# Attention followed by a mixture of experts on one core: a new order of loads, deferred VectorE work and smaller preparation steps

## Chip, cores, metric

One core of one Trainium2 chip. The metric is the device time of one execution in microseconds (us). Every profile is one execution, and its span is about 1.8 us shorter than the time reported for the same run. In the lines of the profile PE is TensorE, PEld its weight loads, DVE VectorE, ACT ScalarE, POOL GpSimd, and SP the engine that only issues transfers; a `q` behind a name means its queue. An eviction is the copy or sum that takes a product out of the banks that TensorE writes. "Loss" below means this, for any stretch: the start-to-start distances of the matmuls that the trace records, minus what these matmuls take at their usual pace (216 ns for 256 columns, 109 ns for 128, 54.5 ns for the half-size ones). That pace sums to 1198.4 us over the whole kernel, before and after alike.

## The reference, cut

```python
def _attn_ref(q, k, v, lam):                    # (4, 8, 768, 64) each; lam (8,)
    for b in range(nb):                         # blocks of 64 positions, with a running state
        intra = np.einsum('bhic,bhjc->bhij', qb, kb) * Dmask[None]
        intra = np.einsum('bhij,bhjd->bhid', intra, vb)
        inter = np.einsum('bhid,bhde->bhie', qb * lam_pow[None], kv_state)
        out[:, :, sl] = intra + inter
        kv_state = lam_block[None, :, None, None] * kv_state + np.einsum('bhsd,bhse->bhde', kb_dec, vb)

def _moe_ref(x, domain_probs, w1, w2):          # x (3072, 512); w1 (4, 512, 1024); w2 (4, 1024, 512)
    p = domain_probs / (domain_probs.sum(-1, keepdims=True) + 1e-09)
    for e in range(E):
        h = np.maximum(x @ w1[e], 0.0)
        out += p[:, e:e + 1] * (h @ w2[e])
```

## The kernel before

Attention runs in 24 chunks of 128 positions, eight to a group. A chunk has three parts: `turn` (transposes of q and k), `scores`, and `values` (with the update of the state `kv`). The experts' products use seven half-size products in place of eight (M1 to M7), so sums of blocks of x and of the weights have to be made first. For the first two experts of group 0 these products work straight from SBUF (`direct_product`, four "quarters" each). For all others the operands are made by GpSimd (group 0's x by VectorE) and ScalarE's queue stores them in DRAM ahead of time ("chores"); SP's queue loads them back (`xs_in`, `ws_in`). VectorE sums that are not urgent wait in a list, `background`, and one is issued after each part of a product.

The parts that the change touches (cuts marked `...`):

```python
    def load(n):
        ...
        for name, src in (("q", q), ("k", k), ("v", v)):
            x = small(f"{name}n")[:].rearrange("p (h d) -> p h d", d=D)
            nc.sync.dma_start(out=x, in_=src[b, :, c * C:(c + 1) * C, :].rearrange("h p d -> p h d"))
    ...
    lam_bc = consts.tile([P, H], FP32, name="lam_bc")
    nc.scalar.dma_start(out=lam_bc[:], in_=lam.partition_broadcast(P))
    lam_hp = consts.tile([P, NHP], FP32, name="lam_hp")
    for hd in range(2):
        nc.scalar.dma_start(
            out=lam_hp[half[hd], :], in_=lam.rearrange("(hp hd) -> hd hp", hd=2)[hd].partition_broadcast(D),
        )
    ...
    def pump():                                  # one chore; stores of the chore before are issued first
        for f in stores:
            f()
        stores.clear()
        if chores:
            chores.pop(0)()

    def inner(eng, what, to, blk, ops, at):      # the sums of one operand, then three stores
        ...
        stores.append(lambda: (
            nc.scalar.dma_start(out=to[:, 0], in_=blk[:, 0, 0:256]),
            nc.scalar.dma_start(out=to[:, 1:5], in_=s[:]),
            nc.scalar.dma_start(out=to[:, 5:7], in_=blk[:, 1].rearrange("p (a f) -> p a f", a=2)),
            made.add(what),
        ))
    ...
    for n in range(4):
        load(n)
    for name in ("A21", "A22", "A11"):
        raw_w1(0, name)
    probs = consts.tile([P, NTOK // P, E], FP32, name="probs")
    nc.scalar.dma_start(out=probs[:], in_=moe_domain_probs.rearrange("(t p) e -> p t e", p=P))
    ...
    # in values(): the state, at once after its product
            for hd in range(2):
                ...
                    tt(nc.vector, kv[sl, :, sl], kv[sl, :, sl], q_decay[...], ALU.mult)
                    tt(nc.vector, kv[sl, :, sl], kv[sl, :, sl], kpv[sl, :, sl], ALU.add)
    ...
    # in first_product(): an eviction, then (as a later step) the sums that wait in background
            at, begins = READ[i]
            if not begins:
                tt(nc.vector, new[at][:], p[:], new[at][:], ALU.add)
            elif old is None:
                nc.scalar.copy(out=new[at][:], in_=p[:])
            else:
                tt(nc.vector, new[at][:], p[:], old[at][:], ALU.add)
    ...
    # in second_product(): the result of the last expert, 128 x 512
            if e == E - 1 and m in ("M5", "M3"):
                nc.gpsimd.dma_start(out=out[n * P:(n + 1) * P, :], in_=acc.pop(n)[0][:])
    ...
    # the main loop, after each of four parts x of a pair of products (cut)
                rest()
                ...
                if x in (1, 4, 6):
                    pump()
```

Of the kernel before, what the change touches and what calls it, by code (L numbers as in the profile page):

```python
# [20 lines left out]
def kernel(  # L21
# [36 lines left out]
    C = P  # L58
# [39 lines left out]
    def load(n):  # L98
        b, c = divmod(n, NCH)
        tiles = []  # L100
        for name, src in (("q", q), ("k", k), ("v", v)):
            x = small(f"{name}n")[:].rearrange("p (h d) -> p h d", d=D)
            nc.sync.dma_start(out=x, in_=src[b, :, c * C:(c + 1) * C, :].rearrange("h p d -> p h d"))  # L103
            tiles.append(x)
        nat[n] = tiles
# [3 lines left out]
    lam_hp = consts.tile([P, NHP], FP32, name="lam_hp")  # L109
    for hd in range(2):  # L110
        nc.scalar.dma_start(
            out=lam_hp[half[hd], :], in_=lam.rearrange("(hp hd) -> hd hp", hd=2)[hd].partition_broadcast(D),
        )
# [56 lines left out]
    def prepare_w1(e):  # L170
        st = {}

        def block(name, i, j):
            t = stage.tile([P, 2, W], FP32, name="w1b", tag="st")
            src = moe_w1[e, j * 256:(j + 1) * 256, i * W:(i + 1) * W]
            nc.sync.dma_start(out=t[:], in_=src.rearrange("(c p) f -> p c f", p=P))
            st[name] = t

        def total(name, a, b, op):
            t = stage.tile([P, 2, W], FP32, name="w1o", tag="st")  # L180
            tt(nc.gpsimd, t[:], st[a][:], st[b][:], op)
            st[name] = t

        def ready(m):
            inner_w1(e, m, st[A_OF[m]])

        return [
            lambda: (block("A11", 0, 0), block("A21", 1, 0), block("A22", 1, 1)),
            lambda: ready("M1"),
            lambda: (total("S1", "A21", "A22", ALU.add), ready("M5")),  # L190
            lambda: (total("S3", "A11", "A21", ALU.subtract), ready("M7")),
            lambda: (total("S2", "S1", "A11", ALU.subtract), block("A12", 0, 1), ready("M6")),
            lambda: ready("M2"),
            lambda: (total("S4", "A12", "S2", ALU.subtract), ready("M3")),
            lambda: ready("M4"),
        ]
# [39 lines left out]
    def prepare_x(g):  # L236

        st = {}

        def total(name, a, b, op):  # L240
            t = stage.tile([P, 2, W], FP32, name="xo", tag="st")
            tt(nc.gpsimd, t[:], a, b, op)
            st[name] = t[:]

        def ready(m, blk):
            inner_x(nc.gpsimd, g, m, blk)

        return [lambda: ready("M1", b11), lambda: ready("M2", b21)], [
            lambda: (total("T1", b12, b11, ALU.subtract), ready("M5", st["T1"])),
            lambda: (total("T2", b22, st["T1"], ALU.subtract), ready("M6", st["T2"])),  # L250
            lambda: (total("T3", b22, b12, ALU.subtract), ready("M7", st["T3"])),
            lambda: ready("M3", b22),
            lambda: (total("T4", b21, st["T2"], ALU.subtract), ready("M4", st["T4"])),
        ]
# [29 lines left out]
    for n in range(4):  # L284
        load(n)
    for name in ("A21", "A22", "A11"):
        raw_w1(0, name)
    probs = consts.tile([P, NTOK // P, E], FP32, name="probs")
    nc.scalar.dma_start(out=probs[:], in_=moe_domain_probs.rearrange("(t p) e -> p t e", p=P))
# [16 lines left out]
    nc.vector.tensor_copy(out=q_decay[:, :, 0], in_=lam_hp[:])  # L306
# [11 lines left out]

    gate = consts.tile([P, NTOK // P, E], FP32, name="gate")
# [15 lines left out]

    def turn(n, tags):
        qn, kn, _ = nat[n]
# [11 lines left out]
        if n % NCH:  # L349
            qs = small("qs")  # L350
            tt(nc.vector, qs[:], qT[:], q_decay[:].rearrange("p h c -> p (h c)"), ALU.mult)
# [7 lines left out]
    def scores(n, tags):  # L359
        qT, kT, _ = turned[n]  # L360

        sp = [bank(tags[hd], "sp") for hd in range(2)]
        for hp in range(NHP):
            for hd in range(2):
                nc.tensor.matmul(  # L365
                    out=sp[hd][:, hp * C:(hp + 1) * C], lhsT=hc(kT)[half[hd], hp], rhs=hc(qT)[half[hd], hp],
                    start=True, stop=True,
                )
        st = [small("st") for _ in range(2)]
        for hd in range(2):  # L370
            tt(nc.vector, st[hd][:], sp[hd][:], s_decay[:, hd].rearrange("p h c -> p (h c)"), ALU.mult)
        masked[n] = st

    def values(n, tags):
        _, kn, vn = nat.pop(n)
# [18 lines left out]
        if not last:  # L394
# [7 lines left out]
            for hd in range(2):  # L402
                sl = half[hd]
                if first:
                    nc.vector.tensor_copy(out=kv[sl, :, sl], in_=kpv[sl, :, sl])
                else:
# [4 lines left out]
                    tt(nc.vector, kv[sl, :, sl], kv[sl, :, sl], kpv[sl, :, sl], ALU.add)  # L411

# [21 lines left out]
    background = []  # L434

    def rest(n=1):
        for _ in range(min(n, len(background))):
            background.pop(0)()

# [134 lines left out]
    def second_product(g, e, m, banks):  # L574

        def part(sj, s):
# [29 lines left out]
            if e == E - 1 and m in ("M5", "M3"):  # L606
                nc.gpsimd.dma_start(out=out[n * P:(n + 1) * P, :], in_=acc.pop(n)[0][:])  # L607
# [16 lines left out]
    def direct_product(e, m, blocks, tags):  # L624
# [6 lines left out]
        def quarter(at):  # L631
# [9 lines left out]
            new[at] = small("m" + at) if m in ("M1", "M2", "M5") else blocks[old][at]  # L641
            if old is None:
                nc.scalar.copy(out=new[at][:], in_=p[:])
            else:
                tt(nc.vector, new[at][:], p[:], blocks[old][at][:], ALU.add)
# [7 lines left out]
    between, blocks = [], {}  # L653
    for i in range(CPG + 2):
        if i == 3:
            sum_w1(0, "S1", "A21", "A22", ALU.add)
            sum_w1(0, "S3", "A11", "A21", ALU.subtract)
        if i == 4:
# [3 lines left out]
        if i > 4:  # L662
            pump()
        if i == 6:
            between = direct_product(0, "M1", blocks, ("g1", "g3"))
        for f, lag in ((scores, 1), (turn, 0), (values, 2)):
# [3 lines left out]
            if i == 7 and lag == 0:  # L670
                between += direct_product(0, "M2", blocks, ("g1", "g3"))
            if between:
                between.pop(0)()
        if i + 4 < CPG:
            load(i + 4)
        if i == 0:
            raw_w1(0, "A12")
        if i == 6:
            gates()

    def sum_x(name, a, b):
        t = stream.tile([P, 7, 256], FP32, name="xt", tag="xw"[len(x_now) % 2])
        x_now[name] = t[:, 0:4].rearrange("p (c a) t -> p c (a t)", c=2)
        tt(nc.vector, x_now[name], x_now[a], x_now[b], ALU.subtract)

    sum_x("T1", "B12", "B11")
    sum_x("T2", "B22", "T1")
    sum_x("T3", "B22", "B12")
    sum_x("T4", "B21", "T2")
    for f in between:  # L690
        f()
    chores.extend(lambda n=n: raw_w1(1, n) for n in ("A11", "A12", "A21", "A22"))
    chores.append(lambda: sum_w1(1, "S1", "A21", "A22", ALU.add))
    for m in SEQ0[2:]:
# [9 lines left out]
        lambda: sum_w1(1, "S3", "A11", "A21", ALU.subtract), own[1], w2_steps[0],  # L704
        lambda: sum_w1(1, "S4", "A12", "S2", ALU.subtract), own[2], w2_steps[1],
        own[3], w2_steps[2], w2_steps[3], own[4], w2_steps[4], w1_steps[0], own[5], *w1_steps[1:3], own[6], *w1_steps[3:],
# [6 lines left out]
    for at, (g, e) in enumerate(units):  # L713
# [9 lines left out]
        for i in range(7):  # L723
# [11 lines left out]
            for x, part in enumerate(order):  # L735
# [10 lines left out]
                if x in (1, 4, 6):  # L746
                    pump()
    assert not (background or chores or stores or acc)
# [28 lines left out]
```

## Time and profile before

| | before |
|---|---|
| time, median of 3 runs | 1261.21 us (1259.52 to 1261.83) |
| span of the profile | 1257.4 us |
| matmuls at their usual pace | 1198.4 us |
| first matmul starts | 4.69 us |
| loss before 120 us | 24.8 us |
| loss from 120 to 720 us | 24.8 us, of which TensorE idle 9.7 |
| last matmul's start to the end | 5.3 us |

Read it from the top: TensorE is the bound, so a change that doesn't touch the matmuls can win only what the last four rows hold, and not all of that.

### The profile page before, as it was taken

The numbers are of one execution on the slowest core, as the hardware profiler recorded it, in microseconds if no ns is written. First come the engines' busy times: TensorE is split into PE (matmuls) and PEld (weight loads), VectorE is DVE, ScalarE is ACT, GpSimd is POOL, SyncE is SP. The second block draws the span as 40 slices with busy tenths as digits, with TensorE's granted clock in tenths as the row PEclk, the third lists the DMA queues.
The fourth block names the chain that finished last, engine by engine and source line by source line (L and its number), as shares of the span: only waits on it lengthen the run. The fifth ranks groups of instructions, "written<-read, shape, count | busy, mean of one in ns | idle before, by whom it ended". The sixth has DMA issues, their size and how long they took to land.

```text
span 1257.4 us, 16224 instructions
## 1 busy us (share of the span) xinstructions
PE 1226.8 (98%) x6376; PEld 1071.3 (85%) x6376; DVE 762.4 (61%) x1267; ACT 217.1 (17%) x361; POOL 301.1 (24%) x294
## 2 busy tenths in 40 slices
PE   6989999999999999999999999999999999999998
PEld 5878888888888888888888888888888888888887
DVE  4656478477467745756764674674764755755742
ACT  2213102111202211220221021120120120220100
POOL 3620236586356683112000700000010000000001
PEclk9999999999999999999999999999999999999999
DMA  9741477999999799667544764454565445454412
GB/s 187 209 151 47 166 251 270 374 317 382 307 341 348 225 328 362 214 222 237 176 176 151 265 232 177 175 202 154 217 224 199 178 174 203 154 217 156 167 59 93
DMA packets 173052, 273.10 MB, mean 217 GB/s; under 512 B 87600, under 2 KB 120496, under 8 KB 172976
## 3 DMA queue, kind: packets, MB, share of 16 engines
q1 hardware_dynamic: 143808, 212.37, 50.6%
q10 hardware_dynamic: 27248, 53.41, 11.3%
q0 software_dynamic: 1920, 6.29, 1.3%
q8 instruction: 50, 0.82, 0.3%
q14 instruction: 26, 0.21, 0.1%
HBM read 212.39 MB, written 59.64 MB: 216 GB/s over the span
## 4 chain that ended last, share of the span: by engine, by line
PE 47%; issue 42%; DMA 5%; POOL 2%; SPq 2%; DVE 1%; ACT 0%; ACTq 0%; POOLq 0%; DVEq 0%
PE q L589 18%; PE pg L537 14%; PE pM L637 7%; PE op L389 2%; PE sp L365 2%; PE kvp L398 2%; SPq L103 1%; PE op L383 1%; DMA xs_in<-x_ops 1%; DMA x_ops<-xo 1%; DMA w2t<-in_moe_w_dram 1%; POOL ops L93 1%; POOL out_dram L607 1%; PE qp L342 1%; DMA kn<-in_k_dram 1%
## 5 line engine op out<-in xcount | busy, mean ns | idle before, releaser
L537 PE MATMUL pg<-xs_in,ws_in 128*128 128x256 f32 x1960 | 470.9, 380 | 6.6 <-DVE m L93 3.4
L537 PEld LDWEIGHTS pg<-xs_in,ws_in 128*128 128x128 f32 x1960 | 369.2, 190 | 60.3 <-DVE m L93 5.6
L589 PE MATMUL q<-w2t,hS 128*128 128x256 f32 x1536 | 361.0, 379 | 0.0
L93 DVE TENSOR_TENSOR m<-pg,m 128x512 f32<-128x512 f32 x410 | 280.1, 688 | 92.9 <-PE pg L537 79.2
L589 PEld LDWEIGHTS q<-w2t,hS 128*128 128x128 f32 x1536 | 291.1, 190 | 39.9
L605 DVE SCALAR_TENSOR_TENSOR acc<-q,gate,acc 128x256 f32<-128x256 f32 x288 | 138.9, 482 | 234.6 <-PE q L589 234.2
L589 PE MATMUL q<-w2t,m 128*128 128x256 f32 x1152 | 270.7, 379 | 0.0
L589 PEld LDWEIGHTS q<-w2t,m 128*128 128x128 f32 x1152 | 218.5, 190 | 29.7
L607 POOL DMA_DIRECT2D out_dram<-acc x24 | 13.2, 550 | 548.6 <-DVE acc L605 548.6
L549 ACT ACTIVATE m<-m 128x512 f32<-128x512 f32 x120 | 75.4, 630 | 361.9 <-DVE m L93 349.7
L93 DVE TENSOR_TENSOR hS<-m,m 128x512 f32<-128x512 f32 x96 | 68.8, 719 | 20.9 <-ACT m L549 20.9
L545 ACT COPY m<-pg 128x512 f32<-128x512 f32 x80 | 46.5, 585 | 174.9 <-PE pg L537 157.1
L93 DVE TENSOR_TENSOR m<-m,m 128x512 f32<-128x512 f32 x96 | 73.8, 773 | 0.0
L93 POOL TENSOR_TENSOR kn<-kn,s_decay 128x256 f32<-128x256 f32 x40 | 30.1, 773 | 114.1 <-PE kp L342 110.9
L491 ACT ACTIVATE m<-m 128x512 f32<-128x512 f32 x48 | 29.9, 629 | 152.3 <-DVE m L93 147.7
L637 PE MATMUL pM<-xt,w1o 128*128 128x256 f32 x192 | 45.6, 391 | 4.8 <-DVE xt L93 3.3
L637 PEld LDWEIGHTS pM<-xt,w1o 128*128 128x128 f32 x192 | 37.2, 196 | 10.7 <-DVE xt L93 3.5
L602 DVE TENSOR_SCALAR acc<-q,gate 128x256 f32<-128x256 f32 x48 | 23.1, 482 | 37.2 <-PE q L589 37.1
L93 DVE TENSOR_TENSOR m<-pM,m 128x512 f32<-128x512 f32 x40 | 27.4, 687 | 24.9 <-PE pM L637 24.8
L93 DVE TENSOR_TENSOR st<-sp,s_decay 128x512 f32<-128x512 f32 x48 | 30.8, 684 | 11.4 <-PE sp L365 11.2
L93 DVE TENSOR_TENSOR hS<-hS,m 128x512 f32<-128x512 f32 x48 | 35.3, 736 | 0.5
L93 POOL TENSOR_TENSOR w2o<-w2b 128x1024 f32<-128x1024 f32 x8 | 18.9, 2364 | 69.4 <-DMA w2b<-in_moe_w_dram 49.9
(65 smaller groups left out, 777.4 us busy)
## 6 DMA issues: line engine op xcount, KB each, us to landing
xs_in<-x_ops SPq DMA_DIRECT2D x70, 896.0 KB, 4.6
ws_in<-w_ops SPq DMA_DIRECT2D x70, 896.0 KB, 6.6
w2t<-w_sums SPq DMA_DIRECT2D x96, 256.0 KB, 6.4
w2t<-in_moe_w_dram SPq DMA_DIRECT2D x72, 256.0 KB, 6.6
w_ops<-ops ACTq DMA_DIRECT2D x28, 512.0 KB, 6.8
x_ops<-ops ACTq DMA_DIRECT2D x21, 512.0 KB, 5.0
w2b<-in_moe_w_dram SPq DMA_DIRECT2D x32, 256.0 KB, 5.6
w_sums<-w2o ACTq DMA_DIRECT2D x16, 512.0 KB, 6.7
```

Source lines behind the costliest of these rows:

```text
L93: eng.tensor_tensor(out=o, in0=a, in1=b, op=op)
L365: nc.tensor.matmul(out=sp[hd][:, hp * C:(hp + 1) * C], lhsT=hc(kT)[half[hd], hp], rhs=hc(qT)[half[hd], hp], start=True, stop=True,)
L389: nc.tensor.matmul(out=op[half[hd], hp * C:(hp + 1) * C], lhsT=vn[:, 2 * hp + hd], rhs=hc(st[hd])[:, hp], start=(first and hp == 0), stop= ...
L398: nc.tensor.matmul(out=kpv[:, hp], lhsT=kn[:, 2 * hp:2 * hp + 2].rearrange("p h d -> p (h d)"), rhs=vn[:, 2 * hp:2 * hp + 2].rearrange("p ...
L491: nc.scalar.activation(out=o[:], in_=o[:], func=AF.Relu)
L537: nc.tensor.matmul(out=p[:, j * 256:(j + 1) * 256], lhsT=ws[:, W1_AT[i], j * P:(j + 1) * P], rhs=xs[:, X_AT[i]], start=(fresh and j == 0), ...
L545: nc.scalar.copy(out=new[at][:], in_=p[:])
L549: nc.scalar.activation(out=new[at][:], in_=new[at][:], func=AF.Relu)
L589: nc.tensor.matmul(out=p[:, s * DH:(s + 1) * DH], lhsT=h[A_OF[m]][:, c * 256 + s * P:c * 256 + (s + 1) * P], rhs=fed2[g, e, m][uu][:, c], ...
L605: nc.vector.scalar_tensor_tensor(out=o, in0=x, scalar=w, in1=o, op0=ALU.mult, op1=ALU.add)
L607: nc.gpsimd.dma_start(out=out[n * P:(n + 1) * P, :], in_=acc.pop(n)[0][:])
L637: nc.tensor.matmul(out=p[:, s * 256:(s + 1) * 256], lhsT=a[c][:, f:f + P], rhs=b[:, c, j * 256:(j + 1) * 256], start=(s == 0 and c == 0), ...
```

## The change

The intent has five parts, named as in the prediction:

- (a) **Loads.** The small strided load `lam_hp` goes (its values are copied from `lam_bc`), `probs` is loaded later, and q and k of the first two chunks come ahead of v.
- (b) **Early quarters.** The quarters of M1 and M2 are spread over the first attention group from the fifth chunk on, so that one is left to run behind the eighth chunk, while VectorE forms the sums of x.
- (c) **`soon`.** VectorE's masks, `qs` and state updates are put at the head of the deferred list, so that the next eviction is ahead of them. (For the first eight chunks they still run at once.)
- (d) **Steps.** Preparation sums and operands become separate chores, and a chore is asked for (a "pump") four times per product in place of three; most of group 0's own operands come ahead of the w2 sums.
- (e) **Results** are stored by halves, the last four halves from SP's queue.

```diff
-    lam_hp = consts.tile([P, NHP], FP32, name="lam_hp")
-    for hd in range(2):
-        nc.scalar.dma_start(
...
-            lambda: (total("T1", b12, b11, ALU.subtract), ready("M5", st["T1"])),
+            lambda: total("T1", b12, b11, ALU.subtract), lambda: ready("M5", st["T1"]),
... (every sum and its operand in the same way)
-    for n in range(4):
-        load(n)
-    for name in ("A21", "A22", "A11"):
-        raw_w1(0, name)
-    probs = consts.tile([P, NTOK // P, E], FP32, name="probs")
-    nc.scalar.dma_start(out=probs[:], in_=moe_domain_probs.rearrange("(t p) e -> p t e", p=P))
+    for n, names in ((0, "qk"), (1, "qk"), (0, "v"), (2, "qk"), (1, "v")):
+        load(n, names)
+    raw_w1(0, "A11")
+    load(3, "qk")
... (v2, A12, v3, A21, A22)
+    def soon(n, *work):
+
+        background[0:0] = work
+        if n < CPG:
+            rest(len(work))
...
-            tt(nc.vector, qs[:], qT[:], q_decay[:].rearrange("p h c -> p (h c)"), ALU.mult)
+            soon(n, lambda: tt(nc.vector, qs[:], qT[:], q_decay[:].rearrange("p h c -> p (h c)"), ALU.mult))
... (the two masks and the two state updates in the same way)
-            if e == E - 1 and m in ("M5", "M3"):
-                nc.gpsimd.dma_start(out=out[n * P:(n + 1) * P, :], in_=acc.pop(n)[0][:])
+            if e == E - 1 and m in ("M2", "M4", "M5", "M3"):
+                queue = nc.sync if (g, m) == (NG - 1, "M3") else nc.gpsimd
+                queue.dma_start(out=out[n * P:(n + 1) * P, j * DH:(j + 1) * DH], in_=o)
...
+    m1, m2 = (direct_product(0, m, blocks, ("g1", "g3")) for m in ("M1", "M2"))
+    between = {
+        4: (m1[0], m1[2]), 5: (m2[0], m2[2]), 6: (m1[1],), 7: (m1[3],), 8: (m2[1],), 9: (lambda: None, lambda: None, m2[3]),
+    }
...
+            if i == 9 and lag == 2:
+                x_sums()
...
+        if i == 5:
+            nc.scalar.dma_start(out=probs[:], in_=moe_domain_probs.rearrange("(t p) e -> p t e", p=P))
+        if i == 9:
             gates()
...
-        lambda: sum_w1(1, "S3", "A11", "A21", ALU.subtract), own[1], w2_steps[0],
-        lambda: sum_w1(1, "S4", "A12", "S2", ALU.subtract), own[2], w2_steps[1],
-        own[3], w2_steps[2], w2_steps[3], own[4], w2_steps[4], w1_steps[0], own[5], *w1_steps[1:3], own[6], *w1_steps[3:],
+        lambda: sum_w1(1, "S3", "A11", "A21", ALU.subtract), own[1], own[2],
+        lambda: sum_w1(1, "S4", "A12", "S2", ALU.subtract), own[3], own[4], *w2_steps[:2], own[5], *w2_steps[2:], own[6],
+        *w1_steps,
...
-                if x in (1, 4, 6):
+                if x % 2 == 0:
                     pump()
```

## The prediction

> **What bounds the kernel now.** I read the page's head and slices first, then busy times by stretch, then the timeline wherever TensorE was idle, and last every matmul's start.
>
> ```profile
> span 1257.4 us, 16224 instructions
> PE 1226.8 (98%) x6376; PEld 1071.3 (85%) x6376; DVE 762.4 (61%) x1267; ACT 217.1 (17%) x361; POOL 301.1 (24%) x294
> PE   6989999999999999999999999999999999999998
> ```
>
> TensorE is busy 98% of the span and the loss sits in the first slices. A busy record can still hide a slow matmul, so I also compared the start-to-start distance of all 6376 records with the distance that most have: 216 ns for 256 columns (8 records take 1.73 us in the chain), 109 ns for 128 columns, 54.5 ns for each of the half-size ones, of which two run side by side. That sum is 1198.4 us. The rest of the 1257.4: 4.7 us before the first matmul, 24.8 us lost before 120 us, 24.8 us between 120 and 720, nothing after 720, and 5.3 us from the last matmul's start to the end (these sum to 1258.0; from 720 on the nominal is 0.6 too high). So there are four places to look at. The change's number of matmuls and their shapes are the same (1356 rows in both listings), so it can win only here.
>
> Busy times by stretch: TensorE, weight loads, VectorE, ScalarE, GpSimd, clock, DMA share, GB/s.
>
> ```profile
> 0.00:20.00 20.00, 9.91 (x55) 7.82 (x56) 8.22 (x22) 3.86 (x6) 3.10 (x10) 1.00 0.90 139
> 112.00:720.00 608.00, 598.28 (x3255) 520.54 (x3254) 381.66 (x623) 106.54 (x180) 249.14 (x236) 1.00 0.76 264
> 720.00:1258.00 538.00, 532.47 (x2468) 468.39 (x2466) 315.33 (x536) 81.24 (x132) 13.66 (x21) 1.00 0.48 176
> ```
>
> **Start.** The timeline (start, length, work; the idle time before it in brackets):
>
> ```profile
> 4.69 1.09 PE L342 MATMUL qp<-ident,qn 128*128 128x128 f32 x4 [4.69 <-DMA qn<-in_q_dram]
> 7.38 1.11 PE L342 MATMUL kp<-ident,kn 128*128 128x128 f32 x4 [1.60 <-DMA kn<-in_k_dram]
> 13.65 1.12 PE L342 MATMUL qp<-ident,qn 128*128 128x128 f32 x4 [2.40 <-DMA qn<-in_q_dram]
> 29.97 0.63 PE L342 MATMUL qp<-ident,qn 128*128 128x128 f32 x4 [1.29 <-DMA qn<-in_q_dram]
> ```
>
> Transfers issued in the first 25 us (KB each, us to landing):
>
> ```profile
> probs<-in_moe_domain_probs_dram ACTq DMA_DIRECT2D x1, 48.0 KB, 10.1
> lam_hp<-in_lam_dram ACTq DMA_DIRECT2D x2, 1.0 KB, 6.7
> ```
>
> TensorE waits for inputs. The packet records say why: from 5 to 8 us the loads' queue moves only some 50 to 110 packets per us, beside 110 four-byte packets per us of lam_hp; from 9 to 11 us probs puts through about 2,900 sixteen-byte packets; from 14 us on the loads get 850 per us, one q, k or v tile (1024 packets) each 1.2 us. Until about 19 us each transpose also takes 213 ns, twice the 107 of later.
>
> **After the eighth chunk**, and **the middle:**
>
> ```profile
> 72.05 1.72 DVE L93 TENSOR_TENSOR xt<-xT 128x1024 f32<-128x1024 f32 x1
> 73.82 6.49 PE L637 MATMUL pM<-xt,w1o 128*128 128x256 f32 x21 [3.28 <-DVE xt L93]
> 420.46 0.42 DVE L93 TENSOR_TENSOR kv<-kv,kvp 64x256 f32<-64x256 f32 x1
> 421.66 1.99 PE L537 MATMUL pg<-xs_in,ws_in 128*128 128x256 f32 x8 [0.90 <-DVE m L93]
> 443.57 0.58 ACT L545 COPY m<-pg 128x512 f32<-128x512 f32 x1 [5.55 <-DMA x_ops<-xo]
> 444.20 1.99 PE L537 MATMUL pg<-xs_in,ws_in 128*128 128x256 f32 x8 [2.24 <-ACT m L545]
> ```
>
> TensorE stands 3.28 us until VectorE has built the first token sum. At 421 the eviction of a first product stands behind VectorE's state update. At 443 it stands in ScalarE's queue behind operand stores: store, wait for an earlier landing, copy. There are nine such gaps from 112 to 720: 1.49 (161), 0.11 (220), 0.85 (237), 1.67 (308), 0.33 (376), 0.90, 2.24, 1.81 (484), 0.33 (545), together 9.7 us, plus some 0.1 to 0.16 us each for the first exposed weight load: 11 us. The other 14 us of the middle's 24.8 are the attention blocks' own switching costs, which stay.
>
> **What the Trainium skill says.** "TensorE: Matmul & The Clock Gate", Part 1: the array starts throttled, needs about 3.4 us of sustained work for the full clock and falls back after an idle window. The trace agrees: 213 ns at the start, and after the 3.28 us pause eight matmuls at 402 to 427 ns in place of 216 after a slow first one; the clock column says 1.00 at the start all the same. The same page (the table at its head) calls the queues of ScalarE and VectorE strict FIFOs: the rows at 421 and 443 are that. "DMA: Bandwidth & Descriptors", Anatomy of one DMA: a DMA's semaphore wait happens on the issuing sequencer; that is why a store on ScalarE's queue holds up the copy behind it (5.55 us here). Same page, Specifications: first byte about 1 us for GpSimd's path against 0.6 for SP's; the trace has 2.29 us from issue to landing for the last store, and 1.70 at best for a small store issued from ScalarE.
>
> **The change, part by part.**
>
> (a) Loads. lam_hp goes, probs moves to about 25 us, q and k of two chunks come first. At 1.2 us a tile after the first landing at 4.56: k0 5.8, q1 7.0, k1 8.2, v0 9.4, q2 10.6, k2 11.8, v1 13.0; with half a weight block per 0.75 us (the landings from 24.8 to 27.7) A11 14.5, q3 15.7, k3 16.9, v2 18.1, A12 19.6, v3 20.8, A21 and A22 23.8, q4 25.0, k4 26.2. TensorE, with block lengths from before: q0 4.7 to 5.8, k0 to 6.8, copy of kT 0.58, scores 7.4 to 9.5, second transposes to 11.2, copy, scores from 11.9. If the clock opens near 12: scores to 13.0, third transposes to 14.0; first values at 14. They began at 20.28. If it opens only at 15, at 15.5. Call it 14.6: 5.7 us. Then scores 1.1, transposes 0.9, values 3.1 and the early quarters (1.73 each) follow; the fifth chunk comes after the first quarter, at about 24.5, and waits some 1.5 us for k4 (before: 1.29 + 0.45 for chunk 4 and 0.87 later for the next, 2.6). Saved up to the last state product: 5.7 + 1.1 = **6.8 us**.
>
> (b) One quarter of M2 (1.73 us) now stands behind the eighth chunk, while VectorE works on the sums. The pause of 3.28 becomes about 1.5 (1.8 saved); a pause that short should not throttle the array, which saves the 8 x 0.21 + 0.1 = 1.8. **3.6 us.** The gates' small operations, now later, run behind the sums with 6.9 us of M5 to hide in.
>
> (c) `soon` puts masks, qs and state updates at the head of the deferred list, so the next eviction is in front of them. VectorE's operations are the same in number and length. It ends the gaps at 376, 421 and 545: 1.6 + 3 x 0.12 = 2.0 us.
>
> (d) Smaller steps, pumped four times per product (13 us) in place of three. GpSimd's work for sum plus operands is 2.36 + 4 x 0.8 = 5.6 us, more than the old interval of 4.3; now it is 2.4 or 3.2 against 3.25. From 417.8 to 445.6 GpSimd ran without a break, 28 us for five steps that were asked for in 22; nine steps at 3.25 are 29. So stores are issued less far ahead of their data and in smaller bursts, and less often block ScalarE: the gaps at 237, 308, 444, 484 (6.6 + 0.5). The one at 161 is VectorE's: 8.2 us for the landing of a w2 sum before it can build operands; their order changes too, most of them now ahead of the w2 steps. I take 55% of these 8.7: 4.8 us. Against this 0.5 us for new collisions. (c) and (d): **6.3 us**.
>
> (e) Half-width stores; the last on SP's queue. After the last VectorE result (1252.99): no 0.30 us of GpSimd start, 0.6 less to landing, and GpSimd's closing drain, which ended 1.03 us after the landing, starts earlier: **1.3 us**. The 24 more issues (0.55 us each) lie on an idle GpSimd late, and in group 0's last unit beside preparation: they cost nothing on the path.
>
> Sum 6.8 + 3.6 + 6.3 + 1.3 = 18.0. 1261.2 - 18.0 = **1243.2 us**, 1.4% less.
>
> **Rivals.** First: in the middle the wait only moves. Landings of stores take 5 to 9 us at 264 GB/s, and bytes and their order change little; earlier chores make SP wait longer for staging buffers (it stood up to 10.6 us at 434), and then operands come late. For it: ScalarE's waits at 237, 444 and 484 end with a landing, not with GpSimd. Against: fewer stores per us, and SP's feeds run a product ahead. The middle then gains 0 to 2: 1248. Second: the start is bound by weights and the cold clock. If the loads run no faster without the small packets, or the clock opens late, (a) gives 3: 1247. Third: VectorE's delayed masks reach the values step late, or the late probs collides with loads at 25 us: new waits of 1 to 3 us; both rivals and this one together give about 1254. In the other direction: all gaps gone, (a) 9, (b) 4.4, (c) and (d) 10, (e) 2: 1236.
>
> **Range and chances.** The parts err by about 2, 1, 3.5 and 0.7 us; their root sum is 4.2, and I widen for unseen collisions: 1236 to 1251. Faster by over 2% needs below 1236, that is 25.2 of at most some 29 us that could be had (21.1 of waits after the first matmul's, 3 of weight loads and restart, 3 of cold clock, 2 of tail): 6%. Slower by over 2% needs 25 us of new waits in a stream with no fewer buffers: 1%.
>
> **What would show it.** Right: second q transposes by 8 to 10 us; matmuls at 107 ns from 12 to 15 us; first sum product at 63 to 67 in place of 73.8 with under 2 us of idle before it and no 427 ns matmuls; TensorE idle from that to its last third 3 to 6 us in place of 9.7, with none before it by a state update; last landing to end shorter. Wrong: idle still about 10 us in the middle, with SP or landings as releaser; or a first product that starts at 70.

## The result, and the profile after

| | before | after |
|---|---|---|
| time, median of 4 runs each | 1260.37 us (1258.76 to 1261.83) | 1241.37 us (1240.46 to 1243.29) |
| ratio | | 0.9852, 95% interval 0.9833 to 0.9870 |
| span of the profile | 1257.4 us | 1241.5 us |
| first values block | 20.28 us | 15.94 us |
| first product with a sum of x | 73.82 us | 65.66 us |
| loss up to about 115 us | 24.8 us | 14.9 us |
| loss in the 600 us after it | 24.8 us | 19.9 us |
| of which TensorE idle | 9.7 us | 4.4 us |
| last matmul's start to the end | 5.29 us | 4.18 us |

A ratio here and below is the mean time of one kernel's runs over the mean of the other's in the same rounds, so it is not quite the ratio of the medians quoted. A gain in us is (1 - ratio) x 1260. The profiled execution of the changed kernel was the slowest of its four: its span was 1241.5, the others' 1238.7 to 1240.0. So the profile shows up to 3 us less than the gain in time.

The head and the TensorE row of the slices, after:

```profile
span 1241.5 us, 16264 instructions
PE 1225.3 (99%) x6376; PEld 1074.6 (87%) x6376; DVE 761.6 (61%) x1268; ACT 216.9 (17%) x361; POOL 309.1 (25%) x314
PE   8999999999999999999999999999999999999998
```

The gain is at the start of the row and in what the tenths can't show: same matmuls, same VectorE work, 16 us less span. Busy times by stretch, after (the stretch, then TensorE, weight loads, VectorE, ScalarE, GpSimd, clock, DMA share, GB/s):

```profile
0.00:20.00 20.00, 13.89 (x100) 11.81 (x101) 10.74 (x27) 5.38 (x8) 4.83 (x12) 1.00 0.88 213
104.00:712.00 608.00, 603.63 (x3277) 527.56 (x3276) 384.61 (x629) 107.57 (x181) 254.22 (x248) 1.00 0.77 266
```

In the first 20 us DMA moves 213 GB/s where it moved 139, and TensorE gets 100 matmuls done where it did 55. In the middle the idle time falls from 9.7 to 4.4 us. The timeline of the start, after (start, length, engine, line, work; idle time before it in brackets):

```profile
4.76 1.09 PE L355 MATMUL qp<-ident,qn 128*128 128x128 f32 x4 [4.76 <-DMA qn<-in_q_dram]
7.38 2.08 PE L378 MATMUL sp<-qT,kT 64*128 64x128 f32 x16 [0.68 <-ACT kT L361]
9.39 1.11 PE L355 MATMUL qp<-ident,qn 128*128 128x128 f32 x4
15.94 1.46 PE L405 MATMUL op<-st,vn 128*64 128x128 f32 x16
```

The only idle times left are two of 0.68 us for ScalarE's copy of kT. But the blocks still take 1.1 and 2.1 us, twice what they take later: by the distances of the matmuls' starts, the array has its full pace only from 16.8 us on. And the small transfers of the first 40 us (KB each, us from issue to landing):

```profile
probs<-in_moe_domain_probs_dram ACTq DMA_DIRECT2D x1, 48.0 KB, 4.6
lam_bc<-in_lam_dram ACTq DMA_DIRECT2D x1, 4.0 KB, 3.0
```

`probs` lands in 4.6 us at its new place where it took 10.1. The loads' queue now moves 850 to 1070 packets per us from 4 to 11 us. Before, it moved 46 to 112 per us from 5 to 8 us, beside `lam_hp`'s four-byte packets, and 230 to 660 from 9 to 12, beside those of `probs`; from 12 us on it moved 810 to 890.

The end of the first attention group, after:

```profile
58.73 0.87 DVE L421 COPY kv<-kvp 64x256 f32<-64x256 f32 x2 [1.42 <-PE kvp L414]
59.76 1.13 PE L399 MATMUL op<-qs,kv 128*128 128x128 f32 x8 [1.06 <-DVE kv L421]
62.84 1.89 PE L650 MATMUL pM<-xT,w1b 128*128 128x256 f32 x8
64.37 1.23 DVE L93 TENSOR_TENSOR xt<-xT 128x1024 f32<-128x1024 f32 x1
65.66 4.58 PE L650 MATMUL pM<-xt,w1o 128*128 128x256 f32 x20 [0.93 <-DVE xt L93]
```

A quarter (62.84) now covers part of the first sum (64.37), and the pause of 3.28 us is 0.93; the matmuls after it run at 216 ns, none at 427. But there is a wait that was not there before: 1.06 us at 59.76. The seventh chunk's state product was followed by a quarter before, which gave VectorE time to copy the state; now the eighth chunk's values come next and wait for that copy.

Two waits of the middle, after. First the largest, near 213 us:

```profile
212.55 0.33 ACTq L141 DMA_DIRECT2D w_ops<-ops  x1
213.67 0.33 ACTq L142 DMA_DIRECT2D w_ops<-w1b  x1
214.04 0.58 ACT L557 COPY m<-pg 128x512 f32<-128x512 f32 x1 [6.45 <-DMA w_ops<-ops]
214.67 3.67 PE L549 MATMUL pg<-xs_in,ws_in 128*128 128x256 f32 x8 [2.53 <-ACT m L557]
```

ScalarE's copy stands behind two stores in its own queue; the second of these can't be issued until an earlier transfer that uses the same completion semaphore has landed (at 213.65, issued at 204.76). So ScalarE is idle for 6.45 us with a copy at hand, and TensorE for 2.53. This is the kind of wait that the prediction showed at 444, at another place; before, TensorE waited only 0.10 us here (at 220). Second, a small one near 417, of the kind that (c) was to end:

```profile
413.02 2.35 POOL L93 TENSOR_TENSOR xo<-xT,xo 128x1024 f32<-128x1024 f32 x1
413.37 2.55 DVE L93 TENSOR_TENSOR hS<-m,m 128x512 f32<-128x512 f32 x1
416.98 1.48 DVE L93 TENSOR_TENSOR m<-pg,m 128x512 f32<-128x512 f32 x2
417.71 1.99 PE L549 MATMUL pg<-xs_in,ws_in 128*128 128x256 f32 x8 [0.35 <-DVE m L93]
```

The state update is gone from ahead of the eviction (416.98), and a deferred sum `hS` stands there instead, with two short operations behind it. It took 2.55 us, where most (172 of 192) take 0.67 to 0.70, because GpSimd's sum of 2.35 us had begun 0.35 us before it: it finished 0.55 us after GpSimd's end. The same thing stretched the state update of the kernel before:

```profile
417.79 2.35 POOL L93 TENSOR_TENSOR xo<-xT 128x1024 f32<-128x1024 f32 x1 [15.08 <-ACT xT L393]
418.64 1.79 DVE L93 TENSOR_TENSOR kv<-kv,q_decay 64x256 f32<-64x256 f32 x1
```

An operation that takes 0.42 us elsewhere took 1.79, to 0.3 us after GpSimd's end at 420.14. The excess of 1.37 us is more than the wait of 0.90 us that followed. The Trainium skill says this plainly ("SBUF — State Buffer", section "SBUF: two separate sides"): a VectorE operation with two SBUF inputs and a GpSimd operation that reads SBUF take one shared pair of ports as an exclusive lock, for the whole instruction, and whichever is later blocks. Both traces agree.

### The profile page after: what moved, and what is told of

It is laid out like the page before. It is cut to its first block, busy times and chain, and to the rows that moved or that the text cites. A ratio compares the mean times of both kernels' runs of the same rounds, so it can differ in the third digit from the quotient of the medians.

```text
span 1241.5 us, 16264 instructions
## 1 busy us (share of the span) xinstructions
PE 1225.3 (99%) x6376; PEld 1074.6 (87%) x6376; DVE 761.6 (61%) x1268; ACT 216.9 (17%) x361; POOL 309.1 (25%) x314
## 4 chain that ended last, share of the span: by engine, by line
PE 90%; DMA 3%; POOL 3%; DVE 2%; issue 0%; ACT 0%; SPq 0%; POOLq 0%; ACTq 0%; DVEq 0%
PE q L601 43%; PE pg L549 34%; PE pM L650 5%; PE sp L378 2%; PE op L405 2%; POOL ops L93 2%; PE kvp L414 2%; PE op L399 1%; DMA w_ops<-ops 1%; PE qp L355 1%; PE kp L355 1%; DMA w2b<-in_moe_w_dram 1%; DVE hS L93 1%; POOL w2o L93 1%; POOL w1o L93 1%; DVE m L93 1%
## 5 line engine op out<-in xcount | busy, mean ns | idle before, releaser
L620 POOL DMA_DIRECT2D out_dram<-acc x44 | 24.1, 548 | 545.9 <-DVE acc L617 545.9
L93 DVE TENSOR_TENSOR hS<-m,m 128x512 f32<-128x512 f32 x96 | 73.3, 768 | 13.2 <-ACT m L561 13.2
L93 DVE TENSOR_TENSOR m<-m,m 128x512 f32<-128x512 f32 x96 | 70.5, 739 | 0.0
```

The lines of the kernel that those rows point to most:

```text
L93: eng.tensor_tensor(out=o, in0=a, in1=b, op=op)
```

## The experiments

Twelve kernels ran, each beside runs of the kernel before; all gave correct results. Theory before the first: the start earns some 10 us by (a) and (b), mostly by the loads; (c) and (d) earn the rest. The rivals: the start earns little by itself; `soon` or the steps only move waits.

| kernel | median us | ratio to before (95%) | gain us | loss to ~115 | loss of the middle |
|---|---|---|---|---|---|
| before | 1260.37 | | | 24.8 | 24.8 |
| after | 1241.37 | 0.9852 (0.9833 to 0.9870) | 18.6 | 14.9 | 19.9 |
| e1_packets | 1256.05 | 0.9975 (0.9960 to 0.9990) | 3.2 | 19.7 | 26.5 |
| e2_start | 1245.55 | 0.9901 (0.9883 to 0.9918) | 12.5 | 15.0 | 25.7 |
| e3_soon | 1264.21 | 1.0033 (1.0019 to 1.0048) | -4.2 | 25.6 | 26.6 |
| e4_steps | 1251.78 | 0.9949 (0.9934 to 0.9964) | 6.4 | 26.0 | 18.9 |
| u_soon | 1241.77 | 0.9853 (0.9834 to 0.9872) | 18.5 | 13.5 | 20.1 |
| u_steps | 1248.97 | 0.9918 (0.9899 to 0.9937) | 10.3 | 14.5 | 25.7 |
| u_quarter | 1242.06 | 0.9855 (0.9838 to 0.9873) | 18.3 | 16.5 | 17.0 |
| x_poolstores | 1252.39 | 0.9941 (0.9924 to 0.9958) | 7.4 | 15.1 | 30.9 |
| u_order | 1240.99 | 0.9848 (0.9824 to 0.9871) | 19.2 | 14.2 | 21.5 |
| t_tail | 1241.53 | one run, state unknown | | 14.0 | 16.9 |
| b1_both | 1238.23 | 0.9824 (0.9804 to 0.9844) | 22.2 | 11.7 | 18.0 |
| b2_spaced | 1237.60 | 0.9819 (0.9799 to 0.9838) | 22.8 | 11.0 | 18.4 |

The last two columns are from one profile each. They move by up to 3 us between runs of the same code (the middle of t_tail is the changed kernel's: 16.9 against 19.9), so differences of that size in them are no finding.

**e1_packets: the small packets alone, in the kernel before.**

```diff
-    lam_hp = ...                                  (and its two loads; q_decay is copied from lam_bc)
-    probs = ...; nc.scalar.dma_start(out=probs[:], ...)
...
+        if i == 5:
+            nc.scalar.dma_start(out=probs[:], ...)
-        if i == 6:
+        if i == 9:
             gates()
```

> The kernel before with one thing changed: lam_hp's two transfers are gone (its values are taken from lam_bc) and the load of probs moves behind the sixth chunk; the order of the q, k, v and weight loads stays. My theory: the tiny packets held up the loads. Then q1 lands near 8 us in place of 13.6, the second q transposes start near 9.4 in place of 13.65, the first values near 16 in place of 20.3, the first product of a token sum near 69 to 70 in place of 73.8, and the kernel gains 4 to 5 us (ratio 0.996 to 0.997). Rival: the order of the loads and the place of the quarters do it, and the packets are short enough to be hidden; then q1 lands after 12 us and the gain is under 1.5 us.

Measured: 3.2 us in time. But the start did what (a) was to do. The first values came at 14.05 us, and the last state product at 62.14 where it was at 69.38, with the same eight quarters ahead of it: 7.2 us, for the 6.8 that (a) forecast with its new order too. (In this profile the array had its full pace early, from 12.2 us on; see below.) So the packets alone bring about the whole of (a). `lam_hp` and `probs` went together; which of them matters more was not tried. Where the gain went shows in its timeline:

```profile
65.29 0.25 DVE L320 TENSOR_REDUCE total<-probs 128x24 f32<-128x96 f32 x1
66.51 1.22 DVE L93 TENSOR_TENSOR xt<-xT 128x1024 f32<-128x1024 f32 x1
67.78 2.50 PE L634 MATMUL pM<-xt,w1o 128*128 128x256 f32 x5 [4.48 <-DVE xt L93]
```

My edit put the gates' small operations (65.29 to 66.5) ahead of the first sum of x, so TensorE paused 4.48 us, and the 11 or so matmuls after it ran at about 427 ns. That was a fault of the experiment, some 1.2 us more of pause than before (4.48 for 3.28) and 0.9 us of slow matmuls (11 for 8). The middle lost 1.7 us more than before, which is within what this figure moves by.

**e2_start: (a) and (b) alone.** The changed kernel with `soon` made to run at once, and with steps, order of chores and stores as before.

```diff
-        background[0:0] = work
-        if n < CPG:
-            rest(len(work))
+        for f in work:
+            f()
...
-            lambda: total("T1", ...), lambda: ready("M5", st["T1"]),      (all sums so)
+            lambda: (total("T1", ...), ready("M5", st["T1"])),
...
-                if x % 2 == 0:
+                if x in (1, 4, 6):
                     pump()
```

> The whole start part alone (loads, lam_hp, probs, early quarters, a quarter behind the token sums); VectorE's attention work, preparation steps and stores as before. My theory: TensorE's losses up to 120 us fall from 24.8 to about 15 us as in the changed kernel and the rest stays as before: first sum product at 65 to 66 us, idle in the middle 8 to 11 us, total 10 us less (ratio 0.992). Rival: the gains of the parts depend on each other, since an earlier first part shifts GpSimd's work against TensorE's; then the middle changes by over 3 us and the total is off by as much.

Measured: 12.5 us in time. In its profile the start has lost 15.0 us against 24.8 (9.8 us), and the middle 25.7, as before. The start is worth 10 to 12 us by itself, and no effect of it on the middle is seen.

**e3_soon: (c) alone, in the kernel before.**

```diff
-            tt(nc.vector, qs[:], qT[:], q_decay[:]..., ALU.mult)
+            soon(n, lambda: tt(nc.vector, qs[:], qT[:], q_decay[:]..., ALU.mult))
... (masks and state updates so)
```

> The kernel before with masks, qs and state updates of the later chunks put at the head of the deferred list, and nothing else. My theory: gaps of TensorE that VectorE's in-order queue makes (376, 421 and 545 us, 1.6 us together) go; ScalarE's gaps (237, 308, 444, 484) stay within 2 us: middle idle near 8 us in place of 9.7, 1 to 3 us gained (ratio 0.998 to 0.999). Rival: the deferred order frees ScalarE too, since its relu waits for VectorE; then the ScalarE gaps shrink as well and the gain is 4 us or more.

Measured: slower, by 4.2 us (the interval excludes 1). My expectation of a gain fell. What costs the 4.2 us is not shown. The largest wait in its timeline, near 310 us:

```profile
308.23 0.33 ACTq L147 DMA_DIRECT2D w_ops<-ops  x1
310.09 0.59 ACT L360 COPY kT<-kp 128x512 f32<-128x512 f32 x1
310.73 1.89 PE L377 MATMUL sp<-qT,kT 64*128 64x128 f32 x16 [4.47 <-ACT kT L360]
```

A wait of 1.67 us at this place became 4.47: the copy of kT stood behind ScalarE's stores, and these behind an earlier landing (an operand load of SP's queue that took 7.5 us). The waits at 376, 421 and 545 that `soon` was meant to end came back elsewhere. But TensorE's idle time in the middle is 9.9 us against 9.7, so the longer wait is balanced by shorter ones. The middle lost 26.6 us against 24.8, which is within what this figure moves by; the start 25.6 against 24.8, where `soon` runs its work at once and so changes nothing.

**e4_steps: (d) alone, in the kernel before.** The sums and operands as separate chores, the new order, four pumps.

```diff
-            lambda: (total("T1", ...), ready("M5", st["T1"])),      (all sums so)
+            lambda: total("T1", ...), lambda: ready("M5", st["T1"]),
...
-                if x in (1, 4, 6):
+                if x % 2 == 0:
                     pump()
```

> The kernel before with the small preparation steps, four pumps per product and the new order of the first preparations, and nothing else. My theory: stores on ScalarE's queue stand less in front of copies; ScalarE's and the operand gaps fall from 8.2 to about 3 us, 3 to 5 us gained (ratio 0.996 to 0.998). Rival: landings of stores, not GpSimd's backlog, set those gaps; then the middle idle stays within 2 us of 9.7 and the total within 1.5 us.

Measured: 6.4 us; the middle's loss falls from 24.8 to 18.9, its idle time from 9.7 to 4.6, and the start stays. So (d) is what earns in the middle. It is three edits in one (separate chores, four pumps, a new order), and no run tells which of them earns.

**u_soon: the changed kernel without `soon`** (its work is run at once: the first hunk of e2_start).

> The changed kernel with only the putting-behind undone: masks, qs and state updates are issued where they stood before. My prediction gave it 2.0 us: then this run is 2 us slower than the changed kernel (1243 to 1244) and has gaps of 0.3, 0.9 and 0.3 us by VectorE near 367, 413 and 537. After the run with soon alone (4.2 us slower than before) the rival is that it gains nothing or costs: then this run is within 1 us of 1241 or faster.

Measured: ratio 0.9853 against 0.9852. `soon` earns 0.1 us where it stands. The intervals alone would admit some 2 us either way, but the profile says the same: TensorE's idle time in the middle is 4.5 us against 4.4, and the gaps at 364, 410 and 529 are back with 0.34, 0.89 and 0.33 us, where the changed kernel has others in their place.

**u_steps: the changed kernel without (d)** (the other hunks of e2_start, without the stores).

> The changed kernel with only the preparation steps undone (sum and operands in one step, three pumps per product, old order of the first preparations). Steps alone gained 6.4 us. My theory: the gain is there in both settings; this run takes 1246 to 1249 and has ScalarE gaps of 1 to 4 us near 300, 435 and 475. Rival: with soon in place the steps matter less, since evictions come earlier; then 1242 to 1244.

Measured: 10.3 us of gain in place of 18.6, so (d) earns 8.3 us in its place, and the middle's loss is 25.7 us, as before the change. A single wait of 3.64 us at 211.8, of the same kind as the one at 214.67 above, is the largest in it. Of the expected gaps near 300, 435 and 475, only the one at 436 (1.71 us) came over 1 us.

**u_quarter: no quarter behind the eighth chunk.** M2's two last quarters both come before.

```diff
-        ... 8: (m2[1],), 9: (lambda: None, lambda: None, m2[3]),
+        ... 8: (m2[1], lambda: None, m2[3]),
```

> The changed kernel with one thing moved: the last quarter of M2 goes back between the seventh and the eighth chunk's values, so nothing stands behind the eighth chunk. Theory (b): the wait of 1.06 us for the state copy at 59.8 goes, the pause before the first sum product grows from 0.93 to 2.7 us, and if a pause that long throttles the array, eight matmuls of 320 to 427 ns follow (1.8 us): 2.5 us slower than the changed kernel. Rival: the throttle isn't set off by the pause's length; then all matmuls after it are at 216 ns and the run is 0.5 to 1 us slower.

Measured, in the profile:

```profile
65.43 6.92 PE L650 MATMUL pM<-xt,w1o 128*128 128x256 f32 x23 [2.65 <-DVE xt L93]
```

The pause is back (2.65 us), and with it the slow matmuls: the starts after it are 320 ns apart, then four times 216, then 375, seven at about 427 and one of 267, together 1.8 us lost. But the 1.06 us wait for the state's copy is gone, as a quarter stands there again. In time the two can't be told apart (0.9855 and 0.9852; 0.4 us). The place of that quarter was worth 1.6 us in this profile's start (16.5 against 14.9); in the time nothing is seen, with intervals of some 2 us each.

**x_poolstores: operand stores on GpSimd's queue,** to see whether the waits at 214 end when ScalarE has no stores.

```diff
-            nc.scalar.dma_start(out=to[:, 1:5], in_=s[:]),
+            nc.gpsimd.dma_start(out=to[:, 1:5], in_=s[:]),
... (all four kinds of operand stores)
```

> The changed kernel with the stores of prepared operands (w_ops, x_ops, w_sums) issued from GpSimd in place of ScalarE; everything else as it is. Theory: what is left of the middle's gaps is ScalarE's copies behind stores that wait for an earlier landing; then the ScalarE gaps (2.5 us near 214 in the changed kernel's profile) go, middle idle falls to about 2 us, and the run gains 1 to 3 us. Rival: the 0.55 us that each such issue takes on GpSimd (some 147 of them, 80 us) and its own waits for landings make preparations late; then feeds wait and the run is 2 us or more slower.

Measured: 11 us slower than the changed kernel. The wait near 214 is gone, as the theory had it, but a longer one comes at the feeds:

```profile
244.58 2.04 PE L549 MATMUL pg<-xs_in,ws_in 128*128 128x256 f32 x4 [5.48 <-DMA ws_in<-w_ops]
```

TensorE waits 5.48 us here and 1.5 to 1.9 at four other places. Why is not shown: SP issued the load that ended this wait at 233.46, and it landed 11.0 us later, where the like loads of the changed kernel took 8.0 to 9.7; the last stores of weight operands before it had landed by 225.5. Taking stores off ScalarE in this way is no cure.

**u_order: the changed kernel with the loads in their old order** (q, k, v of a chunk together, then the weights).

```diff
-    for n, names in ((0, "qk"), (1, "qk"), (0, "v"), (2, "qk"), (1, "v")):
-        load(n, names)
... (and the rest)
+    for n in range(4):
+        load(n)
+    for name in ("A11", "A12", "A21", "A22"):
+        raw_w1(0, name)
```

> The changed kernel with the loads back in plain order: q, k, v of four chunks one after the other, then the four weight blocks; lam_hp gone, probs late, early quarters as changed. My theory after the run with the packets alone (first values at 14.0, last state product at 62.1 there with one quarter more in front of it): the small packets were the whole of the start's wait, the order adds nothing. Then this run is within 1 us of the changed kernel and its first sum product starts at 64 to 66 us. Rival: q and k first and weights early are needed for the early quarters; then the first sum product is 2 us or more later.

Measured: ratio 0.9848 against 0.9852, no difference, and the first sum product starts at 64.75. With e1_packets it settles that the packets, not the order, were (a).

**t_tail: the last half-width stores on GpSimd's queue** in place of SP's; one look.

```diff
-                queue = nc.sync if (g, m) == (NG - 1, "M3") else nc.gpsimd
+                queue = nc.gpsimd
```

> The changed kernel with the last half-width stores on GpSimd's queue like the others. Before, 5.29 us from the last matmul's start to the end, after 4.18. If SP's queue is what shortens it (no GpSimd start, shorter way to landing), this run has about 5.2; if the half width is, about 4.2.

Measured: from the last matmul's start to the end 6.51 us, against 5.29 before and 4.18 after; neither expectation met. The last stores, before, after and here (KB, us from issue to landing):

```profile
out_dram<-acc POOLq DMA_DIRECT2D x1, 256.0 KB, 2.3
out_dram<-acc SPq DMA_DIRECT2D x1, 128.0 KB, 1.7
out_dram<-acc POOLq DMA_DIRECT2D x1, 128.0 KB, 2.0
```

With half-width stores on GpSimd's queue the end is worse than with full-width ones by 1.2 us, and SP's queue is what earns: 2.3 us. The data landed even a little sooner than before, but GpSimd's closing drain ended 2.6 us after the landing, against 1.0 before. t_tail is one profile; the five profiles with full-width stores on GpSimd's queue have an end of 5.25 to 5.75 us, the eight with SP's queue one of 3.73 to 4.19.

**b1_both: a version without the two waits that were left.** The first sum of x is issued ahead of the last state update; a quarter stands again between the seventh and eighth chunk's values, another behind them; and the evictions of the first products that were ScalarE copies go to VectorE, so they stand behind no store.

```diff
+            if n == CPG - 1:
+                x_sums(True)                       (T1 only; the others as before)
             soon(n, *(lambda sl=sl: state(sl) for sl in half))
...
-                nc.scalar.copy(out=new[at][:], in_=p[:])
+                nc.vector.tensor_copy(out=new[at][:], in_=p[:])
...
-        ... 8: (m2[1],), 9: (lambda: None, lambda: None, m2[3]),
+        ... 8: (lambda: None, lambda: None, m2[1]), 9: (lambda: None, lambda: None, m2[3]),
```

> The changed kernel with two repairs. Start: M2's second quarter stands between the seventh and eighth chunk's values, its last one behind the eighth, and VectorE builds the first token sum ahead of the last state update: the waits of 1.06 and 0.93 us go, TensorE's loss up to 115 us falls from 14.9 to about 12.5. Middle: evictions of first products that start a sum (L557, ScalarE copies) go to VectorE, so no store on ScalarE's queue stands before them; if ScalarE's queue is the cause of the gap near 214 us (1.5 to 2.9 us in five profiles), it goes, and the total falls by 3 to 5 us to 1237. Rival: VectorE is loaded by 0.69 us per copy and late with its own work in that stage; then new VectorE gaps take its place and the middle stays at 4 us or more.

Measured: 22.2 us of gain, 3.5 more than the changed kernel, though the intervals overlap. The end of the first group in its timeline:

```profile
60.63 1.23 DVE L93 TENSOR_TENSOR xt<-xT 128x1024 f32<-128x1024 f32 x1 [1.88 <-ACT xT L409]
60.87 1.89 PE L652 MATMUL pM<-xT,w1b 128*128 128x256 f32 x8
62.60 1.67 PE L652 MATMUL pM<-xt,w1o 128*128 128x256 f32 x7
```

The sum runs beside the quarter, and the product that needs it starts without any pause. The wait near 214 is gone too; the waits left are of 0.94 us and less. The two repairs were not run apart. In the profile the start loses 11.7 us against 14.9; the middle's 18.0 lies among those of the kernels whose middle is the changed one's (16.9 to 21.5), so what the second repair is worth is not shown.

**b2_spaced: b1_both with the preparation of operands spread a little** (an empty chore before each third one of two experts).

> The same two repairs and the preparation steps of units 1 and 2 spread out by an empty pump after every three. Theory: stores and loads of preparation crowd in the first part of a unit and their landings (6 to 9 us) hold the queues; spread out, the middle idle falls by another 1 us or more. Rival: the landings are set by the bytes of the whole stage (over 300 GB/s from 190 to 400 us), not by the crowding; then nothing changes, within 1 us, or later steps make feeds late by 1 us or more.

Measured: 22.8 us; not to be told apart from b1_both. The idle time of the middle did not fall as the theory had it (4.2 us against 3.4). Its median of 1237.60 is the lowest of all, 3.8 us under the changed kernel; the intervals of their ratios just overlap (0.9799 to 0.9838 against 0.9833 to 0.9870). It was run at another time.

## Why the prediction was right or wrong

The time was right, 1241.4 for 1243.2, inside the range. One of its steps was wrong, (c), and others made up for it: (c) brought 2.0 us less than it said and (d) 1.6 to 3.5 us more. That the sum came so close is partly luck.

- **What bounds it:** right. The span shrank by 15.9 us, and the places named make up all of it: start 9.9, middle 4.9, end 1.1.
- **(a), 6.8 us:** its mechanism, the small packets, is right and shown (e1_packets). The landings came as worked out: k0 5.5 for 5.8, q1 6.5 for 7.0, k1 8.0 for 8.2, v1 12.6 for 13.0, k4 26.8 for 26.2. The last state product moved from 69.38 to 61.84, 7.5 us, of which 1.7 is the quarter that was moved behind it: 5.8. Three terms make the difference of 1. The full pace came at 16.8 us, not at 12 to 15, so the values started at 15.9, not 14.6. The new wait of 1.06 us was in no step. Against these, the wait for the fifth chunk's q and k, put at 1.5 us, did not come. In four other runs of nearly the same start the full pace came at 12.0 to 12.3 us and the values at 13.9 to 14.2; there that wait is 0.5 to 1.4 us, and the first product with a sum of x comes only 0.3 to 1.3 us sooner. The load order, to which the step gave half its text, does nothing (u_order).
- **(b), 3.6 us:** right in kind; 2.35 us of pause and 1.7 of slow matmuls, 4.0 together in the profile. But that it paid in the net is not shown: with the quarter moved back (u_quarter) the time is the same to 0.4 us. The new wait of 1.06 us takes a part of it; by the profiles' starts 1.6 us remain, which the times can neither confirm nor exclude.
- **(a) and (b) together, 10.4 us:** 9.9 in the profile, 12.5 by time when run alone.
- **(c), 2.0 us:** this step failed. "It ends the gaps at 376, 421 and 545": three small gaps came back at 418, 425 and 559 (0.35, 0.73, 0.27 us) in place of 0.33, 0.90 and 0.33. It also said that no wait behind a state update would be left; the one at 559 is that. Alone it cost 4.2 us, in its place it earns 0.1. I had named the operation that stood in front of the eviction and not asked why that operation was late. It was stretched by GpSimd's sum; what stands in its place now is stretched in the same way.
- **(d), 4.8 us:** right in kind, too small. 6.4 us alone, 8.3 in its place. The factor of 55% was a guess, and the gaps that it took as lost were mostly won. That GpSimd's backlog was what made them, as the step argued, no run isolates. What is left is one wait near 210 to 215 of 1.5 to 3.6 us in the variants of the changed kernel that leave stores and copies on ScalarE, of the same kind, where the kernel before had 0.10. With (c) the step said 6.3; the profile shows 4.9 and the times about 8.
- **(e), 1.3 us:** 1.1 measured, for half the reason. SP's queue earned 2.3; the half-width stores that I took to be free cost 1.2 on GpSimd's queue (t_tail, one profile).
- **Rivals:** the first (the wait only moves) was wrong for the steps and right for `soon`. The second was half right: the full pace came late in the profiled run, at a cost of about 1 us, not 4. The third did not come: `probs` landed in 4.6 us.

The parts don't add: 12.5 (e2_start) + 6.4 (e4_steps) - 4.2 (e3_soon) + 1.1 (end) is 15.8, and the whole gives 18.6. The difference is about as large as the errors of the four figures together, some 4 us. It would lie with `soon`, which costs without the steps and not with them: without `soon` the parts sum to 20.0, and u_soon gives 18.5. Why is open; I didn't try it further.

## What to carry to other kernels

Before moving an operation that stands in front of an urgent one, look at its own length against its usual length: here it was stretched by another engine, and so was the next one in its place. Look for tiny packets at the start of a kernel whatever their bytes, as they can hold up all the large loads. And where a compute engine's queue also issues stores, a copy that TensorE needs can stand behind them. The wait of 2.53 us at 214 ended both when the copy went to another engine (b1_both) and when the stores did (x_poolstores), but moving the stores cost 11 us; what moving the copy is worth by itself no run tells.

## What the Trainium skill lacked or had wrong

- "TensorE: Matmul & The Clock Gate", Part 1: it says a window of about 3.4 us of sustained work opens the clock. Here matmuls ran from 4.5 to 4.9 us on, with two gaps of 0.68 us, and the full pace came at 12.0 to 12.3 us in six runs and at 15.8 to 16.8 in five others of nearly the same start. The page does say that the window runs freely and that the count varies; but 7.5 to 12 us before the full pace is far from its figure. Over half of the matmul time in this stretch is transposes (5.8 of 10.7 us in the changed kernel), and no run tells whether these count as work for the clock.
- The same page and part, on falling back: a pause of 2.65 us, less than its window, was followed by slow matmuls, though only after five at full pace (u_quarter). A pause of 0.93 us was not. The fallback cost some 1.7 us there, and 2.6 after a pause of 4.48 us (11 matmuls).
- "DMA: Bandwidth & Descriptors" has no measured case of this: some hundreds of four-byte packets of one queue (`lam_hp`, 1 KB in all) held another queue's loads down to 46 to 112 packets per us where it moves 850 to 1070, and with 3072 sixteen-byte ones after them (`probs`) set the first values back by 4 to 6 us (20.28 against 15.94 and 14.05).
- No page: in this program, as it was built, SP's and ScalarE's DMAs share one set of eight completion semaphores (in the trace's instruction records 165 DMAs of ScalarE and 448 of SP use the same eight, and GpSimd's eight others), and a DMA waits for the semaphore that it is to use; so a store can wait for an unrelated earlier landing before it is issued. ScalarE's copies stood up to 6.45 us behind this.
- No page: what a last store on GpSimd's queue costs beyond its landing. GpSimd's closing drain ended 1.0 us after the landing of a full-width store (five profiles), and 2.6 us after that of a half-width one (one profile).
- "SBUF — State Buffer", section "SBUF: two separate sides", is right as it stands, and it would have corrected step (c): VectorE's operations of 0.42 and 0.69 us took 1.79 and 2.55 beside GpSimd's of 2.35.
